# Pinning the background tasks of a decode step's forward and backward passes to their written place in each engine's order of issue

## The chip, the cores and the metric

The kernel runs on one core of one Trainium2 chip, in a single launch. The metric is the device time of one execution in microseconds (us). Each instruction stands in the queue of one engine (PE for matrix products, DVE for vector work, ACT for scalar work and activations, POOL, and SP, which here only issues transfers), and each engine takes its own queue strictly in the order in which the program was built. Engines wait for each other, and for transfers, by semaphores.

## The reference: what is computed

Two layers, A and B, are applied in turn, twice (A, B, A, B), to one row x of 1024 numbers, and then the gradients of everything are taken by the chain rule from a given `grad_out`. A is attention over a cache, with 32 query heads that share 4 groups of keys and values of 65536 positions each, 128 wide; B is a dense layer with a squared ReLU. Everything is in bfloat16. Cut to what matters:

```python
x = x + A(layernorm(x))      # q = x@wq; softmax(q k^T/sqrt(128)) v; @wo, 8 heads share a group
x = x + B(layernorm(x))      # relu(x@w1+b1)**2 @ w2 + b2
x = x + A(layernorm(x))      # the same caches and weights again
x = x + B(layernorm(x))
out, vjp = jax.vjp(f, x, k_cache, v_cache, wq, wo, w1, b1, w2, b2); grads = vjp(grad_out)
```

The caches are 67 MB each. Their gradients are as large, and are the bulk of what is written; the gradients of wq, wo, w1 and w2 are written too.

## The kernel before

The work over the caches falls into four passes. In passes 1 and 2 (`attn_fwd`) the keys and values are read for the two forward applications of A; in pass 3 (`attn_bwd3`) both are read again for the gradient of the second application; in pass 4 (`attn_bwd4`) they are read once more for the gradient of the first application, and the gradients of both caches, which need the sum over both applications, are formed and written. Between the passes stand the dense layers, which run over slabs of w1 and w2.

A pass goes over 4 groups of 64 items. An item is 8 blocks of 128 positions; four items share one loaded slab of K and one of V (1 MB each). `pipeline` (before: line 453) writes the stages of an item with lags: in pass 4, in round i, `vT` of item i (8 transposes on PE into `ps_tr`, line 875, evacuated by ACT line 151 or DVE line 154), `vS` of item i-2 (8 products into `ps_sc`, line 895; after each four items DVE and POOL form the tile X, lines 902 to 905, and PE transposes it, line 910), and `k8` of item i-7 (8 products for dq, line 932, and four products for the cache gradients, line 938, into the two buffers of `ps_gg`, evacuated by ACT or DVE through `evac` into one of three staging pairs; after four items POOL issues the two output transfers, lines 945 and 946). After the stages of round i, `pipeline` calls the background tasks that the dictionary `bg` holds for i.

The background tasks that matter here, with their written rounds in pass 4:

- `OutGrad.later` forms the dots of 8 rows of wo with a gradient, for a group to come: `dot_va` is a DVE product (line 379) and an ACT sum (line 380). For group 2 (in order) the rounds are 16, 21, ... 51, with rows fetched by SP; for group 3 they are 78, 82, ... 106, with rows fetched by ACT's own queue (line 676) 8 rounds earlier into three row buffers; for group 4 they are 136, 138, ... 150, fetched 4 rounds earlier in the same way.
- `QueryGrad.early` does the same with 8 rows of wq for each of three groups, from rounds 152, 175 and 202 on, with 2.75 rounds from dot to dot and the fetch (line 731) 5 rounds ahead. `QueryGrad.transposed` follows from round 226.
- `rows_ready` (line 1148) clears two row areas with POOL at round 72.
- The weight gradients: `rows_into` (lines 957 to 964) and units of `outer2` (one `ps_gg` buffer each, line 988, and an evacuation), spread evenly over rounds 73 to 252.

In pass 3 there are `OutGrad.later` with slabs that SP loads, `QueryGrad.early` and the transposition of w2; in passes 1 and 2, the rest of the queries and the output products of the groups.

The order that is written is not the order that is issued. A scheduler reorders the instructions when the program is built: it issues what it holds to be ready, the earlier written first, and it keeps only what the data demand. A background task can therefore stand far ahead of its round on an engine's queue. In the built program of before, all 24 steps of `OutGrad.later` in pass 4, with the 16 fetches that ACT issues, stand between instructions 528 and 634 of ACT's order, where pass 4 takes about 528 to 1110; their written rounds are 16 to 150 of 256. Slots for slabs come from `ring`, and a load waits on SP until the slot's last reader is done.

Of the kernel before, what the change touches and what calls it, by code (L numbers as in the profile page):

```python
# [18 lines left out]
def kernel(  # L19
# [22 lines left out]
    out_9: bass.AP,  # L42
):
    nc = tc.nc
    D = A_x.shape[-1]
    G = A_k_cache.shape[1]
    SK = A_k_cache.shape[2]
# [4 lines left out]
    F = B_w1.shape[1]  # L52
    assert DH == P and D == 1024 and QD == 4096 and F % P == 0 and G == 4 and R == 8
    DC, FC = D // P, F // P
    C = SK // P
# [242 lines left out]
    def ln_fwd(x, name):  # L298
# [3 lines left out]
        negmean = tmp.tile([P, 1], F32, name="ln_negmean")  # L302
        nc.vector.tensor_scalar(out=negmean[:], in0=tot[:, :], scalar1=-1.0 / D, scalar2=None, op0=ALU.mult)
        xc = tmp.tile([P, DC], F32, name="ln_xc")
# [6 lines left out]
        rstd = vec.tile([P, 1], F32, name=name + "_rstd")  # L311
        nc.scalar.activation(out=rstd[:], in_=tot2[:, :], func=ACTF.Sqrt, bias=eps_t[:], scale=1.0 / D)
        nc.vector.reciprocal(out=rstd[:], in_=rstd[:])
# [6 lines left out]
    def ln_bwd(dn, n, rstd):  # L320
# [6 lines left out]
        negm = tmp.tile([P, 2], F32, name="lnb_negm")  # L327
        nc.vector.tensor_scalar(out=negm[:], in0=tot[:, :], scalar1=-1.0 / D, scalar2=None, op0=ALU.mult)
        t = tmp.tile([P, DC], F32, name="lnb_t")
# [53 lines left out]
    class RowDots:  # L383
# [12 lines left out]
        def block(self, kc, view):  # L396
# [8 lines left out]
                "C": (L["dve"] + 0.15 * (ng + 1) + N * 0.00053, L["act"], L["pe"] + cpe),  # L405
                "D": (L["dve"] + 0.15, L["act"] + 0.19 * ng + N * 0.00081, L["pe"] + cpe),
            }
# [42 lines left out]
        return ap[:, i * 1024:(i + n) * 1024].rearrange("p (a b) -> p a b", b=P)  # L450


    def pipeline(n, stages, bg=None):
        maxlag = max(l for _, l in stages)
        for i in range(n + maxlag):
            for fn, lag in stages:
                if 0 <= i - lag < n:
                    fn(i - lag)
            for fn in (bg or {}).pop(i, ()):
                fn()  # L460
        assert not bg, sorted(bg)

    def items_of(order):
# [51 lines left out]
    def attn_fwd(L, order, eT, s_areas, more=None, keep=(), have=()):  # L515
# [75 lines left out]
        def v8(idx):  # L591
# [9 lines left out]
            if c8 + 8 == C:  # L601
                sl = slice(g * R, (g + 1) * R)
                nc.vector.tensor_tensor(out=L["oT"][:, sl], in0=ps_o[:, :, 0], in1=L["rZ"][:, sl], op=ALU.mult)
                nc.vector.tensor_copy(out=L["oTb"][:, sl], in_=L["oT"][:, sl])

        pipeline(n, [(kT, 0), (kS, TLEAD), (v8, LAGV)], bg)

    def mlp_hidden(L):
# [156 lines left out]
    def attn_bwd3(L, og, order, eT, dqT, bg):  # L765
# [46 lines left out]
        def k8(idx):  # L812
# [13 lines left out]
            if c8 + 8 == C:  # L826
                nc.vector.scalar_tensor_tensor(out=dqT[:, g * R:(g + 1) * R], in0=ps_dq[:, 0, :], scalar=SCALE,
                                               in1=L["rZ"][:, g * R:(g + 1) * R], op0=ALU.mult, op1=ALU.mult)

        pipeline(n, [(vT, 0), (vS, TLEAD), (k8, TLEAD + UB // 8 + 1)], bg)  # L830

    def attn_bwd4(La, Lb, oga, ogb, order, eTa, eTb, dqT, bg, group_done, streams):
# [82 lines left out]
        def k8(idx):  # L915
# [31 lines left out]
            if c8 + 8 == C:  # L947
                nc.vector.scalar_tensor_tensor(out=dqT[:, g * R:(g + 1) * R], in0=ps_dq[:, 0, 0:R], scalar=SCALE,
                                               in1=La["rZ"][:, g * R:(g + 1) * R], op0=ALU.mult, op1=ALU.mult)
                group_done(order.index(g))  # L950

        pipeline(n, [(vT, 0), (vS, TLEAD), (k8, TLEAD + UB4 // 8 + 1)], bg)


# [281 lines left out]
```

## Time and profile before

| what | us |
|---|---|
| time, median of 3 runs | 2064.12 |
| lowest and highest run | 2061.42, 2067.66 |
| the profiled execution, its own time | 2065.97 |
| its span, first to last instruction | 2064.2 |
| PE, DVE, ACT, POOL busy | 1622.7, 1123.7, 1025.3, 187.8 |
| passes 1 and 2, by the profile about | 12 to 418, 428 to 774 |
| pass 3, about | 832 to 1200 |
| pass 4, about | 1261 to 2040 |

809.62 MB move in all, at a mean of 392 GB/s over the span. The page gives busy time by engine, then the span in 40 equal slices, then the chain of work that ended last: it is followed back from the last instruction, at each step to what released it. A line such as "DVE pair L379 <- DMA pair<-in_A_wo_dram: 20.6, 5, 4.9" says that the DVE instructions of line 379 sat idle 20.6 us in 5 waits, the longest 4.9, until a transfer had landed. In a table of stretches the columns are the stretch, its length, the busy time of PE, its weight loads, DVE, ACT and POOL (instructions in brackets), the granted clock of PE as a share of full speed, the mean busy share of the 16 transfer engines, and the rate that they moved.

### The profile page before, as it was taken

The page shows a single profiled execution, that of the slowest core. Times are in us where ns is not written, and L with a number is a line of the kernel's source. Part 1 is how long each engine was busy: PE and PEld are TensorE (multiplying, and loading weights), DVE is VectorE, ACT ScalarE, POOL GpSimd, SP SyncE. Part 2 cuts the span into 40 slices and gives each one's busy share as a digit, 9 for nine tenths or more (in the row PEclk, how much of TensorE's full clock was granted, in tenths as well). Part 3 has the DMA queues.
Part 4 walks back from the last instruction along what each step waited for, and adds up shares of the span by engine and source line. Part 5 has one row for each costly group of instructions (what it writes and reads, how often), then busy time and mean ns, then how long its engine had stood idle before and what let it go on. Part 6 is the DMA issues. An engine that isn't in the chain of part 4 may idle for free.

```text
span 2064.2 us, 66060 instructions
## 1 busy us (share of the span) xinstructions
PE 1622.7 (79%) x29884; PEld 1332.7 (65%) x29884; DVE 1123.7 (54%) x1817; ACT 1025.3 (50%) x1276; POOL 187.8 (9%) x334
## 2 busy tenths in 40 slices
PE   7888887689888756887787766677888887887886
PEld 7878776578887646877676664455555554555553
DVE  4543431255434304745435557567876766777775
ACT  4543432225433403334435547667665755767764
POOL 0000000000000000000000002112222222222222
PEclk9998997579999955899999977989999988999997
DMA  9999999999999997899999996989999999999996
GB/s 384 419 419 416 414 419 410 390 374 418 415 418 416 400 417 282 359 417 418 416 419 391 413 372 258 362 326 425 424 424 407 405 425 383 398 357 415 394 421 250
DMA packets 142414, 809.62 MB, mean 392 GB/s; under 512 B 14132, under 2 KB 14132, under 8 KB 60980
## 3 DMA queue, kind: packets, MB, share of 16 engines
q1 hardware_dynamic: 108372, 627.12, 75.0%
q0 software_dynamic: 26848, 165.69, 19.6%
q10 hardware_dynamic: 6912, 12.59, 1.7%
q8 instruction: 234, 3.83, 0.7%
q14 instruction: 48, 0.39, 0.0%
HBM read 639.64 MB, written 165.69 MB: 390 GB/s over the span
## 4 chain that ended last, share of the span: by engine, by line
DMA 36%; PE 32%; ACT 15%; DVE 10%; issue 5%; SPq 0%; POOL 0%; ACTq 0%; DVEq 0%; POOLq 0%
DMA slot<-in_A_k_cache_dram 8%; DMA out_dram<-pair 7%; DMA slot<-in_A_v_cache_dram 5%; ACT small L151 5%; PE ps_tr L537 4%; PE ps_sc L556 4%; PE ps_tr L781 3%; DMA pair<-in_A_wq_dram 3%; ACT pair L151 3%; DMA pair<-in_A_k_cache_dram 3%; PE ps_gg L938 3%; PE ps_tr L875 2%; PE ps_acc L599 2%; DMA pair<-in_B_w_dram 2%; DVE small L154 2%
## 5 line engine op out<-in xcount | busy, mean ns | idle before, releaser
L154 DVE COPY small<-ps_tr 128x1024 bf16<-128x1024 bf16 x659 | 444.6, 687 | 347.1 <-PE ps_tr L537 171.9
L151 ACT COPY small<-ps_tr 128x1024 bf16<-128x1024 bf16 x381 | 380.9, 1014 | 415.1 <-PE ps_tr L537 231.7
L151 ACT CAST pair<-ps_gg 128x1024 bf16<-128x1024 f32 x292 | 293.3, 1017 | 164.2 <-PE ps_gg L938 126.1
L154 DVE CAST pair<-ps_gg 128x1024 bf16<-128x1024 f32 x220 | 268.5, 1221 | 80.5 <-PE ps_gg L938 61.0
L938 PE MATMUL ps_gg<-slot,small 64*128 64x512 bf16 x1024 | 199.3, 404 | 72.8 <-DVE pair L154 49.1
L556 PE MATMUL ps_sc<-L_qpad,small 128*128 128x64 bf16 (+7 forms) x3712 | 173.4, 193 | 25.9 <-ACT small L151 11.9
L537 PE MATMUL ps_tr<-ident_b,slot 128*128 128x128 bf16 x2304 | 160.7, 222 | 15.6 <-DMA slot<-in_A_k_cache_dram 13.4
L875 PE MATMUL ps_tr<-ident_b,slot 128*128 128x128 bf16 x1696 | 155.7, 229 | 15.7 <-DVE small L154 10.6
L556 PEld LDWEIGHTS <-small 128*128 128x128 bf16 x3712 | 138.8, 99 | 43.1 <-ACT small L151 20.3
L599 PE MATMUL ps_acc<-eT,slot 128*128 128x64 bf16 x2720 | 131.0, 210 | 38.6 <-DMA slot<-in_A_v_cache_dram 36.6
L875 PEld LDWEIGHTS <-slot 128*128 128x128 bf16 x1696 | 107.9, 102 | 68.1 <-issue 54.8
L537 PEld LDWEIGHTS <-slot 128*128 128x128 bf16 x2304 | 135.0, 99 | 18.7 <-DMA slot<-in_A_k_cache_dram 16.3
L599 PEld LDWEIGHTS <-slot 128*128 128x128 bf16 x2720 | 115.3, 107 | 43.0 <-DMA slot<-in_A_v_cache_dram 40.7
L938 PEld LDWEIGHTS <-small 64*128 64x128 bf16 x1024 | 60.3, 94 | 117.1 <-issue 85.7
L537 PE MATMUL ps_tr<-ident_b,pair 128*128 128x128 bf16 x1600 | 115.8, 226 | 11.3 <-DMA pair<-in_A_k_cache_dram 11.3
L802 PE MATMUL ps_sc<-B_dOpad,small 128*128 128x64 bf16 (+7 forms) x2048 | 102.1, 194 | 23.7 <-ACT small L151 16.1
L895 PE MATMUL ps_sc<-DOB,small 128*128 128x64 bf16 (+3 forms) x2048 | 120.1, 197 | 0.0
L895 PEld LDWEIGHTS <-small 128*128 128x128 bf16 x2048 | 93.1, 101 | 41.7 <-issue 35.1
L537 PEld LDWEIGHTS <-pair 128*128 128x128 bf16 x1600 | 97.1, 102 | 14.6 <-DMA pair<-in_A_k_cache_dram 13.2
L802 PEld LDWEIGHTS <-small 128*128 128x128 bf16 x2048 | 79.1, 100 | 39.0 <-ACT small L151 24.9
L562 DVE TENSOR_REDUCE pm_all<-pair 128x8 f32<-128x512 f32 x64 | 43.9, 686 | 108.0 <-ACT pair L561 108.0
L988 PE MATMUL ps_gg<-pair 128*128 128x512 bf16 x240 | 79.3, 411 | 25.8 <-ACT pair L151 19.5
(265 smaller groups left out, 2392.6 us busy)
## 6 DMA issues: line engine op xcount, KB each, us to landing
slot<-in_A_v_cache_dram SPq DMA_DIRECT2D x172, 1024.0 KB, 13.8
slot<-in_A_k_cache_dram SPq DMA_DIRECT2D x160, 1024.0 KB, 19.6
out_dram<-pair POOLq DMA_DIRECT2D x128, 1024.0 KB, 15.6
pair<-in_A_k_cache_dram SPq DMA_DIRECT2D x81, 1024.0 KB, 19.4
pair<-in_A_v_cache_dram SPq DMA_DIRECT2D x76, 1024.0 KB, 19.8
out_dram<-eT POOLq DMA_DIRECT2D x44, 512.0 KB, 14.9
slot<-in_A_wo_dram SPq DMA_DIRECT2D x16, 1024.0 KB, 10.9
slot<-in_A_wq_dram SPq DMA_DIRECT2D x18, 768.0 KB, 10.5
```

Source lines behind the costliest of these rows:

```text
L151: nc.scalar.copy(out=out, in_=in_)
L154: nc.vector.tensor_copy(out=out, in_=in_)
L537: nc.tensor.transpose(pt[:, i, :], kb8[:, i, :], ident_b[:, :])
L556: nc.tensor.matmul(ps_s[:, slot:slot + w, :].rearrange("p a b -> p (a b)"), lhsT=kt[:, i, :], rhs=L["qpad"][:, g, 0:w, :].rearrange("p a b ...
L562: nc.vector.tensor_reduce(out=pm_all[:, :, c0 // UB], in_=S_sb[:, :, c0:c0 + un], axis=AX.X, op=ALU.max)
L599: nc.tensor.matmul(ps_o[:, :, :].rearrange("p a b -> p (a b)"), lhsT=vb8[:, i, :], rhs=eT[g][:, :, c:c + 8], start=(c == 0), stop=(c == C ...
L781: nc.tensor.transpose(pt[:, i, :], vb8[:, i, :], ident_b[:, :])
L802: nc.tensor.matmul(ps_dp[:, slot:slot + w, :].rearrange("p a b -> p (a b)"), lhsT=vt[:, i, :], rhs=dOpad[:, g, 0:w, :].rearrange("p a b -> ...
L875: nc.tensor.transpose(pt[:, i, :], vb8[:, i, :], ident_b[:, :])
L895: nc.tensor.matmul(ps_dp[:, slot:slot + w, :].rearrange("p a b -> p (a b)"), lhsT=vt[:, i, :], rhs=DOB[:, g, 0:w, :].rearrange("p a b -> p ...
L938: nc.tensor.matmul(pg[:, t2 * 512:(t2 + 1) * 512], lhsT=xt[64 * t2:64 * t2 + 64, blk0 + half, :], rhs=GG[64 * t2:64 * t2 + 64, :, :, :].re ...
L988: nc.tensor.matmul(pg[:, q0:q0 + qq], lhsT=av[:, kb + kk, :], rhs=b_rows[:, n0 + m0 + q0:n0 + m0 + q0 + qq], start=True, stop=True)
```

## The change

A background task is no longer called directly by `pipeline` but through `in_order`. That function notes how many instructions were traced, runs the task, and looks back (over at most 4000 instructions) for the last instruction traced before the task on each engine that the task uses. The first instruction of the task on each such engine gets an edge to that one, of a kind that fixes the order of issue and adds no semaphore wait. The rest of the task, and the stages of later items, are free as before: they may still be issued ahead of the task. No instruction is added or taken away, and every evacuation stays on the engine that it was on.

```diff
+    NOSYNC = mybir.DependencyInfo(mybir.DependencyClass.NoSync, mybir.DependencyReason.DATA)
...
+    def in_order(fn):
+
+        insts = nc.cur_bb.bb.instructions
+        n0 = len(insts)
+        before = {}
+        fn()
+        new = list(insts[n0:])
+        want = {i.engine for i in new}
+        k = n0 - 1
+        while want - set(before) and k >= max(0, n0 - 4000):
+            before.setdefault(insts[k].engine, insts[k])
+            k -= 1
+        for i in new:
+            p = before.pop(i.engine, None)
+            if p is not None:
+                tc.add_manual_dep(i, p.name, NOSYNC, reason="in_order")
+
     def pipeline(n, stages, bg=None):
...
             for fn in (bg or {}).pop(i, ()):
-                fn()
+                in_order(fn)
```

The transfers that a task issues are instructions of the issuing engine's queue, and are pinned with it: the row fetches on ACT's queue, those on SP's, and the clearing on POOL's.

## The prediction, as it was put on record before the result was known

> **What bounds the kernel now.** I read the 40 slices of the page first, then a table of stretches of pass 4, then the chain of waits in the stretch that stood out, then who waited for whom there, and last the order of issue of the two programs as built.
>
> The slices (rows: busy share of the transfer engines, and their rate in GB/s):
>
> ```profile
> DMA  9999999999999997899999996989999999999996
> GB/s 384 419 419 416 414 419 410 390 374 418 415 418 416 400 417 282 359 417 418 416 419 391 413 372 258 362 326 425 424 424 407 405 425 383 398 357 415 394 421 250
> ```
>
> The transfer engines are busy nearly everywhere, at 414 to 425 GB/s when nothing disturbs them. The bytes do not change, so a gain can only come from where the rate is lower: slices 24 to 26, where pass 4 starts, and some of 31 to 39. Passes 1 and 2 have the same order in both programs, so their dips stay.
>
> Pass 4 in stretches (columns: length, busy PE, weight loads, DVE, ACT, POOL with counts, clock, transfer share, GB/s):
>
> ```profile
> 1256.00:1376.00 120.00, 84.85 (x1140) 58.87 (x1139) 79.62 (x130) 82.95 (x108) 25.48 (x37) 0.84 0.78 292
> 1376.00:1480.00 104.00, 85.26 (x1295) 58.32 (x1293) 83.70 (x119) 73.00 (x78) 23.18 (x41) 1.00 1.01 419
> 1480.00:1580.00 100.00, 84.98 (x1089) 55.81 (x1089) 71.29 (x86) 68.14 (x70) 27.30 (x49) 0.97 1.01 424
> 1580.00:1640.00 60.00, 51.88 (x666) 33.81 (x666) 46.97 (x69) 40.27 (x43) 14.40 (x26) 0.94 0.98 393
> 1640.00:1720.00 80.00, 61.23 (x756) 39.88 (x756) 53.41 (x70) 48.34 (x55) 17.01 (x31) 0.90 1.01 424
> 1720.00:1760.00 40.00, 32.45 (x397) 20.97 (x395) 28.68 (x44) 23.98 (x29) 8.94 (x15) 0.86 0.95 370
> 1800.00:1860.00 60.00, 49.94 (x600) 31.52 (x596) 46.25 (x70) 38.56 (x44) 12.85 (x23) 0.89 0.94 352
> 1900.00:1940.00 40.00, 31.77 (x386) 20.11 (x386) 27.42 (x33) 26.95 (x31) 10.72 (x19) 0.91 0.98 385
> ```
>
> From 1376 to 1580 and 1640 to 1720 the rate is at its ceiling, 419 to 424, with DVE and ACT at 60 to 80%: the transfers bound pass 4 there. From 1256 to 1376 they move 292 GB/s with no engine full: something makes all of them wait. The chain of waits names it (start, length, what):
>
> ```profile
> 1293.52 9.53 DMA pair<-in_A_wo_dram
> ...
> 1307.29 7.78 DMA pair<-in_A_wo_dram
> ...
> 1323.36 7.09 DMA slot<-in_A_wo_dram
> ...
> 1333.44 8.20 DMA pair<-in_A_wo_dram
> ...
> 1345.52 10.40 DMA pair<-in_A_wo_dram
> ...
> 1363.30 8.88 DMA slot<-in_A_wo_dram
> ```
>
> Six row fetches of wo, 51.9 us of the 80 from 1296 on. They are fetches of `OutGrad.later` for groups 3 and 4, written for rounds 70 to 146 and issued by ACT right at the start. Only three row buffers exist, so each fetch follows the dot that frees a buffer, and DVE's next dot waits for the fetch. The evacuations queued behind the dot on DVE and ACT wait with it, then PE, then the slots, then the loads. Who waited, from 1256 to 1376 and from 1700 to 2030 (idle us, times, longest):
>
> ```profile
> DVE pair L379 <- DMA pair<-in_A_wo_dram: 20.6, 5, 4.9
> DVE slot L379 <- DMA slot<-in_A_wo_dram: 4.6, 3, 3.8
> ```
>
> ```profile
> DVE pair L379 <- DMA pair<-in_A_wq_dram: 32.0, 8, 5.7
> DVE slot L379 <- DMA slot<-in_A_wq_dram: 4.1, 3, 2.7
> ```
>
> The second pair is the same with the rows of wq, which are hoisted by only a few rounds.
>
> **The change, part by part.** The sum is made against the profiled execution, 2065.97 us (span 2064.2), which is 1.9 above the median of the runs, 2064.12.
>
> *The start of pass 4.* In the new order the 24 wo dots leave positions 528 to 634 of ACT's queue for 550 to 845, that is their written rounds 16 to 150; the 16 fetches on ACT's queue move with them, 4 to 8 rounds ahead of their dots. A round takes about 3.0 us (256 from 1261 to 2030), so a fetch has 12 us or more. The pieces above are 7.1 to 10.4 long: it lands in time, and the waits go. What is late next is the transfers: 120 us at 292 GB/s are 35.0 MB, which at 424 need 82.6, so at most 37.4 can go. Of these, 16.5 lie at 1266 to 1286, where the finer table shows 54 and 95 GB/s: all slots are full and SP waits up to 28.2 us for PE to finish the first slab (line 875). That is compute, not waiting for rows; but ACT is busy 9.5 of 10 us there and six of the dots take 6 x 1.23 of it (1.04 for the sum and 0.19 to read it), so I take 5. From 1296 to 1376 the mean is 334 GB/s, 26.7 MB: 63 us at 424, so 17 can go, and I take 16. The lower end is the time in which the transfer engines were idle from 1296 on, their missing busy shares: 8.9. **Start: -21, bounds -8.9 to -37.**
>
> *The wq dots.* Their order moves later by 3 to 24 places on ACT, so a fetch gets its written 5 rounds, 15 us, where the issue-to-landing row of those fetches says 5.2 to 9.6. The 36.1 us of DVE's waits should go. But transfers ran on beneath most of them. What was lost by rate from 1580 to 2020 is 4.4 + 5.1 + 1.3 + 10.2 + 0.4 + 3.7 + 1.7 = 26.8 (each stretch times 1 minus its rate over 424), of which 20.7 lie between 1720 and 1940. In those stretches PE is busy 79 to 83%, after each wait even above 90%: part of the dip is the catching up, part plain work of the weight gradients (line 964's seven copies, 4.2 us on the chain at 1832), which stays. I take half. **wq: -10, bounds 0 to -26.8.**
>
> *What the dots cost where they land.* 16 dots of 0.69 on DVE and 1.23 on ACT, 30.7 us of engine time, go to rounds 78 to 106 and 136 to 150, about 1495 to 1580 and 1670 to 1710. Both stretches run at 424 GB/s with ACT at 60 to 68%: the transfers hide them. In the second there is a dot every other round, beside the weight gradients, and half of 8 x 1.23 may show. If the cover were gone, all would. **+4, bounds 0 to +30.7.**
>
> *The lag of the cache gradients.* Between items 145 and 217 the new order puts the transposes of `vT` 13 to 15 items ahead of the same item's line 938, where it was 9 to 10, and the dq products 6 to 10 ahead, where it was 2 to 3. K slots come free earlier, outputs go later: 5 items of 0.52 MB, 2.6 MB or 6 us if they could not be caught up; from item 224 the lag is 8 again. **0, bounds -6 to +6.**
>
> *The rest.* `rows_ready` moves from place 22 to 86 on POOL; its 3.5 us memset delays one pair of copies (line 904): 0, at most 3.5. In pass 3 SP issues one 1 MB slab of wo behind four K and V loads instead of before, and eight DVE dots stand some 2 to 15 places later, while the rate is back at 419 from 850 on: 0, within 2 either way. PE's weight-gradient products keep their place among line 938's. No instruction is added.
>
> Sum: -21 - 10 + 4 = -27: 2039 for the profiled execution, **2037** for the median.
>
> A rule of the Trainium skill speaks against the change. The rows: the waits go because fetches are issued later, at round 70 instead of from 1266 us on. "Perfetto Trace Analysis", section "Identifying the Most-Contended Engine", says to find what the engine's gaps wait on and make those dependencies start sooner or finish faster. By it, later fetches would lengthen waits, and the 25.2 us of waits for wo would come back in rounds 70 to 150; by the rows, it is the dots that stand too early, and the waits are gone. The same page, section "Roofline", gives about 120% of 358 GB/s as one core's practical ceiling, an estimate of 430; the trace shows 424 to 425, and by 430 the start could give 38.6 instead of 37.4.
>
> **The rivals.**
>
> *Hidden anyway.* While DVE waited, the transfer engines were 92% busy from 1296 to 1376. If that rate was low because of what was transferred, only the idle share comes back: -8.9 + 4, wq nothing: about 2059 (2054 to 2064). For it: the share; against it: 424 GB/s on the same kinds of load and store right after.
>
> *The dots meet a full chain: slower.* Place: rounds 78 to 150. There each item needs two of the two `ps_gg` buffers and the weight gradients up to one more. If the chain of fill and evacuation is as slow as the transfers, each dot in front of an evacuation holds it for its own time: +30.7, against -21 or only -8.9, and the wq waits stay since their fetches now sit behind the lagging evacuations on ACT: 2074 to 2086, say 2080. It decides once more than about 21 of the 30.7 shows. For it: PE 85% busy there and the lag in the order; against it: ACT 60 to 68%.
>
> *All the lost rate comes back.* -37 and -21 to -27, and some work no longer bunched: 2005 to 2020, say 2010.
>
> That the edges do nothing is excluded by the order: they hold only the first instruction of a task on an engine, but the dots and fetches do move.
>
> **How the numbers follow.** Forecast, 2022 to 2052: 0.60. Hidden: 0.15. Slower: 0.12. All back: 0.13. 0.3% is 6.2 us, about what a measurement here can tell. Faster than 2058: 0.60 + 0.13 + a third of 0.15 = 0.78. Same: the rest of it and a fifth of the slower case: 0.12. Slower: 0.10. The range leaves out the slower case and half of the best: 2015 to 2064.
>
> **What would show it.** Right: no wo row on the chain at the start of pass 4, DVE's waits for wo and wq under some 10 us in all, 400 or more GB/s from about 1290 on, ACT's wo dots spread over rounds 16 to 150. Wrong: waits for wo rows between rounds 70 and 150, rates under 400 there with DVE or ACT above 85%, or wq waits as long as before.

## The result, and the profile after

The changed kernel takes 2049.01 us (median of 4 runs, 2045.81 to 2051.04), the kernel before 2062.77 (4 runs, 2060.91 to 2067.66): a ratio of 0.9928, with a 95% interval of 0.9905 to 0.9951. It is faster by 0.7%. The forecast was 2037, a gain of 1.3%: the direction holds, the range holds the time, and the gain is about half of what was expected. The profiled execution of the changed kernel is its fastest, 2045.81 with a span of 2044.0, and that of before is 3.2 above its median. So the two traces differ by 20.2 us where the medians differ by 13.8; what follows compares traces with traces and medians with medians.

The slices of the page after:

```profile
DMA  9999999999999997899999998799999999989996
GB/s 384 418 419 415 415 419 411 391 372 419 416 418 415 415 404 290 345 419 416 415 420 384 368 383 335 315 424 424 409 419 423 414 417 415 409 353 416 422 420 260
```

Counted from 1 (the prediction counted from 0), slices 25 and 26 (about 1226 to 1329 us) still hold a dip, but from slice 27 on the rate is 409 or more, except in slice 36 and the last. Slices 22 and 23, the end of pass 3, are lower than before: 384 and 368 where they were 391 and 413.

Pass 4 after, in stretches (columns as before: length, busy PE, weight loads, DVE, ACT, POOL, clock, transfer share, GB/s):

```profile
1260.00:1300.00 40.00, 31.62 (x499) 23.65 (x498) 30.02 (x60) 26.70 (x31) 8.23 (x14) 0.88 0.54 209
1300.00:1380.00 80.00, 67.53 (x1071) 46.23 (x1069) 63.19 (x78) 63.34 (x72) 19.99 (x34) 1.00 1.01 419
1380.00:1480.00 100.00, 77.53 (x1082) 52.19 (x1084) 72.36 (x109) 64.20 (x69) 24.38 (x38) 0.95 1.01 417
1480.00:1580.00 100.00, 84.38 (x1104) 55.62 (x1114) 77.56 (x108) 70.19 (x79) 25.02 (x45) 0.95 1.01 421
1640.00:1720.00 80.00, 61.82 (x764) 40.16 (x769) 55.80 (x81) 51.24 (x64) 17.93 (x32) 0.87 1.01 415
1720.00:1820.00 100.00, 81.17 (x1025) 53.53 (x1035) 74.85 (x106) 69.29 (x83) 23.18 (x41) 0.91 1.01 415
1820.00:1840.00 20.00, 18.27 (x200) 11.44 (x202) 17.67 (x29) 10.48 (x13) 3.31 (x5) 0.76 0.66 245
1840.00:1940.00 100.00, 81.59 (x936) 49.94 (x945) 70.42 (x85) 73.58 (x85) 23.23 (x42) 0.86 1.02 419
```

From 1300 to 2000 the transfers run at 414 to 421 GB/s (the stretches not shown, 1580 to 1640 and 1940 to 2000, included), with one hole of 20 us at 1820; behind 2000 the pass runs out. The stretch that moved 334 GB/s before (1296 to 1376) moves 418 now.

The chain of waits after, between 1300 and 1660, its pieces above 9 us (start, length, what):

```profile
1321.10 17.66 DMA out_dram<-pair
...
1348.18 19.96 DMA out_dram<-pair
...
1377.67 21.13 DMA out_dram<-pair
...
1403.18 15.54 DMA slot<-in_A_v_cache_dram
...
1422.46 17.14 DMA slot<-in_A_v_cache_dram
...
1493.03 23.55 DMA out_dram<-pair
...
1528.39 25.36 DMA out_dram<-pair
...
1601.17 23.80 DMA out_dram<-pair
...
1642.42 9.47 DMA pair<-in_A_wo_dram
```

The six fetches of wo that stood at its start are gone. What is there now is the output transfers and the cache loads themselves, which is what a stretch at its ceiling looks like. One row fetch is left, at 1642, beside group 4's dots. DVE's waits for rows, from 1256 to 2030 (idle us, times, longest), are one line:

```profile
DVE pair L380 <- DMA pair<-in_A_wo_dram: 5.9, 1, 5.9
```

There were 25.2 us for wo and 36.1 for wq; none for wq is left.

Where did the rest of the gain go? I timed the passes by the same instructions in both traces: pass 3 from the first transposes of `vT` to the first product that uses the transposed w2, pass 4 from its first transposes to its last product with the transposed wq.

| | pass 3 | gap to pass 4 | pass 4 | span |
|---|---|---|---|---|
| before | 384.0 | 44.8 | 781.4 | 2064.2 |
| after | 391.4 | 42.9 | 756.3 | 2044.0 |
| difference | +7.4 | -1.9 | -25.1 | -20.2 |

The last 0.6 us lie ahead of pass 3 and behind pass 4. Pass 4 gained nearly the 27 that were forecast for it. Pass 3, which I had set at nothing, lost 7.4. There, in the stretch 1080 to 1210, where the dots of wq for three groups stand, the rate fell (columns as above); before:

```profile
1080.00:1210.00 130.00, 98.46 (x1996) 89.14 (x1993) 70.18 (x110) 65.16 (x91) 0.00 (x0) 0.93 1.01 403
```

and after:

```profile
1080.00:1210.00 130.00, 96.38 (x1946) 87.11 (x1944) 65.89 (x98) 63.37 (x87) 0.00 (x0) 0.93 0.96 376
```

27 GB/s over 130 us are 3.5 MB, or 8.3 us at 424: the whole loss of pass 3. No engine does more work. Who made SP, which issues the loads, wait (1090 to 1210) says why; before:

```profile
SPq L248 <- PE ps_tr L781: 37.6, 16, 5.0
SPq L248 <- ACT slot L380: 28.6, 9, 5.2
```

and after:

```profile
SPq L249 <- ACT slot L381: 62.0, 8, 10.1
SPq L249 <- PE ps_tr L799: 13.8, 7, 5.8
```

`QueryGrad.early` in pass 3 takes three dots from one slab of wq, and each dot has a round of its own, two rounds after the last. Before, the three were issued close together: from 1100 to 1200 the third ACT sum of a slab starts 2.1 to 3.0 us after the first. Pinned, it comes four rounds after the first, some 6 us at 1.5 us a round (384.0 over 256); the trace has 6.0 to 9.4. The slab's slot is held until then, the next load that `ring` gives that slot waits at the head of SP's queue, and the loads behind it wait with it. One slab before (start, length, what), first the sums on ACT, then SP's issues:

```profile
1120.11 1.06 ACT L380 ACTIVATE slot<-slot 128x1024 bf16<-128x1024 bf16 x1 [1.36 <-DVE slot L379]
...
1122.06 1.06 ACT L380 ACTIVATE slot<-slot 128x1024 bf16<-128x1024 bf16 x1
...
1123.11 1.04 ACT L380 ACTIVATE slot<-slot 128x1024 bf16<-128x1024 bf16 x1
```

```profile
1118.68 0.33 SPq L248 DMA_DIRECT2D slot<-in_A_wq_dram  x1
1124.27 0.33 SPq L248 DMA_DIRECT2D slot<-in_A_v_cache_dram  x1
...
1125.70 0.50 SPq L248 DMA_DIRECT2D slot<-in_A_k_cache_dram  x1
1129.34 0.33 SPq L248 DMA_DIRECT2D slot<-in_A_v_cache_dram  x1
```

The same after, ACT:

```profile
1119.24 1.06 ACT L381 ACTIVATE slot<-slot 128x1024 bf16<-128x1024 bf16 x1 [1.36 <-DVE slot L380]
...
1121.39 1.06 ACT L381 ACTIVATE slot<-slot 128x1024 bf16<-128x1024 bf16 x1
...
1126.91 1.06 ACT L381 ACTIVATE slot<-slot 128x1024 bf16<-128x1024 bf16 x1
1127.87 0.19 ACT L381 ACTIVATION_READ_ACCUMULATOR slot<-slot 128x1 f32 x1
```

and SP:

```profile
1118.73 0.40 SPq L249 DMA_DIRECT2D slot<-in_A_k_cache_dram  x1
1119.23 0.39 SPq L249 DMA_DIRECT2D slot<-in_A_wq_dram  x1
1128.09 0.33 SPq L249 DMA_DIRECT2D slot<-in_A_v_cache_dram  x1
1128.47 0.90 SPq L1108 DMA_DIRECT2D pair<-in_B_w_dram  x2
1129.46 0.54 SPq L249 DMA_DIRECT2D slot<-in_A_k_cache_dram  x1
1130.10 0.38 SPq L249 DMA_DIRECT2D slot<-in_A_v_cache_dram  x1
...
1140.25 0.33 SPq L249 DMA_DIRECT2D slot<-in_A_k_cache_dram  x1
```

SP issues nothing from 1119.6 to 1128.09, which is 0.03 after ACT has read the sum; then a handful of loads leave within 4 us, and the next comes 8 us later. Before, SP issued something every 1 to 6 us here. That loads leave in bursts, and the transfer engines run dry between them, was a theory at this point. (In the last rounds of the pass the code also takes eight areas out of `ring`, line 1097 of before. Whether a slab held as long would cost anything with those slots still there was not tried.)

### The profile page after: what moved, and what is told of

Same layout as the page of the kernel before. It is cut to its first block, busy times and chain, and to the rows that moved or that the text cites. A ratio compares the mean times of both kernels' runs of the same rounds, so it can differ in the third digit from the quotient of the medians.

```text
span 2044.0 us, 65972 instructions
## 1 busy us (share of the span) xinstructions
PE 1615.9 (79%) x29820; PEld 1327.9 (65%) x29884; DVE 1119.6 (55%) x1817; ACT 1025.1 (50%) x1276; POOL 187.0 (9%) x334
## 5 line engine op out<-in xcount | busy, mean ns | idle before, releaser
L956 PE MATMUL ps_gg<-slot,small 64*128 64x512 bf16 x1024 | 201.5, 405 | 52.0 <-ACT pair L152 15.8
L555 PE MATMUL ps_tr<-ident_b,slot 128*128 128x128 bf16 x2304 | 162.5, 223 | 13.8 <-DMA slot<-in_A_k_cache_dram 11.5
L893 PE MATMUL ps_tr<-ident_b,slot 128*128 128x128 bf16 x1696 | 150.9, 225 | 13.9 <-DMA slot<-in_A_v_cache_dram 11.2
L617 PEld LDWEIGHTS <-slot 128*128 128x128 bf16 x2720 | 115.4, 107 | 42.9 <-DMA slot<-in_A_v_cache_dram 40.0
L381 ACT ACTIVATE pair<-pair 128x1024 bf16<-128x1024 bf16 (+1 forms) x68 | 79.5, 1169 | 33.4 <-DVE pair L380 30.0
## 6 DMA issues: line engine op xcount, KB each, us to landing
slot<-in_A_k_cache_dram SPq DMA_DIRECT2D x160, 1024.0 KB, 13.9
pair<-in_A_k_cache_dram SPq DMA_DIRECT2D x81, 1024.0 KB, 19.2
```

Source lines behind the costliest of these rows:

```text
L381: nc.scalar.activation(out=view, in_=view, func=ACTF.Copy, accum_out=ycol)
L555: nc.tensor.transpose(pt[:, i, :], kb8[:, i, :], ident_b[:, :])
L617: nc.tensor.matmul(ps_o[:, :, :].rearrange("p a b -> p (a b)"), lhsT=vb8[:, i, :], rhs=eT[g][:, :, c:c + 8], start=(c == 0), stop=(c == C ...
L893: nc.tensor.transpose(pt[:, i, :], vb8[:, i, :], ident_b[:, :])
L956: nc.tensor.matmul(pg[:, t2 * 512:(t2 + 1) * 512], lhsT=xt[64 * t2:64 * t2 + 64, blk0 + half, :], rhs=GG[64 * t2:64 * t2 + 64, :, :, :].re ...
```

## The experiments

Each ratio, with its 95% interval, is against the kernel before as it ran beside the experiment. Its median was 2064.57 (11 runs) beside each pass by itself, the wq dots of pass 3 not pinned and the wo dots of pass 4; 2063.21 (11) beside the two with a slab's three dots in one round; and 2062.78 (16) beside the other four.

**Each pass by itself.** The theory: pass 3's pins cost some 7 us and pass 4's bring about 25. The rival: pass 4 gains only the 14 to 20 of the whole, and pass 3's longer time is chance.

```diff
-    def pipeline(n, stages, bg=None):
+    def pipeline(n, stages, bg=None, pin=False):
...
-                in_order(fn)
+                in_order(fn) if pin else fn()
...
-        pipeline(n, [(vT, 0), (vS, TLEAD), (k8, TLEAD + UB4 // 8 + 1)], bg)
+        pipeline(n, [(vT, 0), (vS, TLEAD), (k8, TLEAD + UB4 // 8 + 1)], bg, True)
```

> Only the tasks of pass 4 are pinned; passes 1 to 3 are issued as before. Theory (pass 4 gains 25 us, pass 3 loses 7.4): the loss of pass 3 goes, so about 2037 to 2043 us median, 6 to 8 under the changed kernel's 2049, and the stretch from the first transposes of pass 3 to the products with w2 (pg2) is again 384 us instead of 391. Rival (pass 3's 7 us are chance or come from elsewhere): 2047 to 2051, and that stretch stays near 391.

Measured: 2039.05, 0.9878 [0.9860, 0.9896]. In the trace pass 3 takes 384.1, pass 4 756.6; the rate from 1080 to 1210 is back at 402 GB/s. Its interval lies wholly below that of the changed kernel (0.9905 to 0.9951): this version beats both kernels.

The same edit with `True` in `attn_bwd3` instead:

> Only the tasks of pass 3 are pinned; pass 4 is issued as before. Theory: pass 3 takes 391 instead of 384 us, and nothing else changes: 2068 to 2071 us against 2062.8. Rival (the slip of pass 3 is swallowed by the prefetch at the start of pass 4, or is chance): 2061 to 2065.

Measured: 2076.29, 1.0058 [1.0041, 1.0075]; pass 3 takes 395.9, pass 4 780.6. Pinning pass 3 costs 11.7 us, more than I expected. The two halves, -25.5 and +11.7, make -13.8, which is what the medians of the whole change differ by.

SP's wait for the last reader, in pass 3 alone pinned (1090 to 1210):

```profile
SPq L249 <- ACT slot L381: 68.3, 8, 11.8
```

**Only the wq dots of pass 3 not pinned.** Is it these dots, or the slab of wo and the transposition of w2, which are pinned in pass 3 too?

```diff
-                in_order(fn)
+                fn() if fn in free else in_order(fn)
```

where `free` holds the tasks of `QueryGrad.early` that have no row buffers, which are those of pass 3.

> All tasks pinned as in the changed kernel, except the wq dots of pass 3 (QueryGrad.early with slabs from the ring), which are called directly. Theory: these dots, issued later on DVE and ACT, hold their slab's slot longer, and SP, which must keep its order, waits for that slot with all loads behind it (62 us of waits for ACT's sums in the last group instead of 29). Free again, they give back the 7 us: 2038 to 2044, waits of SP for ACT line 380 near 30 us. Rival (the w2 transposes or the wo slab moved on SP's queue are the cause): 2046 to 2051, waits near 60.

Measured: 2039.53, 0.9881 [0.9864, 0.9897]; pass 3 takes 385.5, and SP waits for ACT 27.9 us. The wq dots alone are the loss of pass 3.

**All pinned, a slab's three dots in one round.** If the loss is the time for which a slab is held, the pins may all stay as long as the third dot comes soon after the first.

```diff
-                    at(bg, i0 + 1 + int((kc * len(gs) + i) * step), lambda kc=kc, i=i: one(kc, i))
+                    at(bg, i0 + 1 + int((kc * len(gs) + (i if rows is not None else 0)) * step), lambda kc=kc, i=i: one(kc, i))
```

> Everything pinned as in the changed kernel, but in pass 3 the three wq dots of one slab are written for the same round instead of two rounds apart, so that the slab's slot is held for a shorter time. Theory (the pins cost pass 3 its 7 us only through the slot that the last dot of a slab holds): pass 3 to the products with w2 takes 383 to 386 us, SP's waits for ACT's sums fall from 62 to near 30, 2038 to 2043. Rival (pinned dots delay the evacuations of pass 3, wherever they stand): 391 us for pass 3, 2046 to 2051.

Measured: 2041.93, 0.9889 [0.9869, 0.9909]; pass 3 takes 383.2, at 402 GB/s from 1080 to 1210. SP's waits there:

```profile
SPq L249 <- PE ps_tr L799: 42.0, 18, 5.7
SPq L249 <- ACT slot L381: 24.9, 9, 4.3
```

ACT's share is back from 62.0 to 24.9 and PE's to 42.0, near the 28.6 and 37.6 of before. The third sum of a slab now starts 2.1 us after the first. SP's waits in all hardly moved (93.3 us before, 89.0 after, 91.5 here); what moved is whether they come in many short pieces or, for two thirds of the time, in eight of up to 10.1 us. The theory is shown: every pin stays, only the hold of the slabs is undone, and the loss is gone.

The same edit with pass 4 alone pinned asks whether there is anything more to have:

> Pass 4 alone pinned, and the three wq dots of a slab of pass 3 written for one round as well. Theory (in the order of before these dots already stand close, the scheduler has moved them forward): the same as with pass 4 alone pinned, 2037 to 2042, pass 3 at 383 to 385. Rival (there is more to gain from slots freed early): under 2036.

Measured: 2040.64, 0.9884 [0.9865, 0.9903]. It is the same as pass 4 alone.

**The parts of pass 4.** Which of its pinned tasks bring the gain? First only the wo dots and their row fetches (`OutGrad.later`, groups 2, 3 and 4, those of group 2 with SP's fetches), nothing else in any pass:

```diff
-                in_order(fn)
+                in_order(fn) if fn in pinned else fn()
```

> Nothing is pinned but the wo dots and their fetches in pass 4. Theory (the start is worth some 16 us, the wq dots and the rest some 9): 2045 to 2050 us, the wo rows gone from the chain at the start of pass 4, DVE's waits for wq rows still near 36 us. Rival (the wo dots alone carry all of pass 4's gain): 2036 to 2041. Rival (they meet a full chain and give it back): 2058 or more.

Measured: 2050.71, 0.9936 [0.9918, 0.9953]; pass 4 takes 768.6, 12.8 less than before. DVE's waits for rows:

```profile
DVE pair L380 <- DMA pair<-in_A_wq_dram: 27.8, 9, 5.5
...
DVE slot L380 <- DMA slot<-in_A_wq_dram: 8.8, 3, 3.4
DVE pair L380 <- DMA pair<-in_A_wo_dram: 6.0, 2, 5.5
```

Then only the wq dots of pass 4, their fetches and the transposition of wq:

> Nothing is pinned but the wq tasks of pass 4 (QueryGrad.early and transposed, with their fetches). Theory (the two hoisted families of rows cost separate stalls; with the wo tasks alone pinned pass 4 was 12 us shorter, with everything 25): the other 10 to 13 us, 2051 to 2056 us, DVE's waits for wq rows near 0, those for wo still near 25. Rival (after the wo stall the slots are refilled, so the wq stalls matter only when the wo stalls are gone, or the pins on the weight gradients do it): 2060 to 2066.

Measured: 2055.21, 0.9960 [0.9948, 0.9972]; pass 4 takes 769.6, 11.8 less.

```profile
DVE pair L380 <- DMA pair<-in_A_wo_dram: 20.9, 6, 7.8
...
DVE slot L380 <- DMA slot<-in_A_wo_dram: 5.1, 2, 4.6
```

Each takes its own waits away, but for 6.0 us of wo, and leaves the other's. 12.8 + 11.8 = 24.6, where pinning all of pass 4 takes 24.8: the pins on the weight gradients and on `rows_ready` give nothing that the traces show. By the medians the two are 13.9 and 7.6, together 21.5 of 25.5, so up to 4 us may be theirs or the measurement's.

**Does the landing of the dots cost ACT time?** To pass 4 alone I added a second, useless ACT sum to each of the 16 wo dots of groups 3 and 4, into a spare column: 16 x 1.25 = 20 us more of ACT in the same rounds.

```diff
+                if queue is nc.scalar:
+                    junk = tmp.tile([P, 1], F32, name="junk")
+                    nc.scalar.activation(out=view, in_=view, func=ACTF.Copy, accum_out=junk[:])
```

> Pass 4 alone pinned, as in the run that gave 2039, and ACT forms the sum of each wo dot of groups 3 and 4 a second time into a spare column: 16 more activations of about 1.2 us, 20 us of ACT, in rounds 78 to 150. Theory of the prediction (the transfers hide the dots where they land, a few us at most show): 2039 to 2045. Rival (the evacuation chain is full there, each dot delays it by its own time): 2053 to 2059.

Measured: 2042.78, 0.9904 [0.9881, 0.9927]. That is 3.7 above pass 4 alone, within the intervals of the two, and pass 4 is 0.7 longer in the trace. ACT had room for it.

**Fetches too close to their dots.** Pass 4 alone, with the fetches of wo 2 rounds and 1 ahead of the dots instead of 8 and 4. This puts the waits for rows where the dots now stand.

```diff
-    og1.later(vbx1, ORD4[2], bg, IPG + 14, 4, wo_rows, 8, nc.scalar)
-    og1.later(vbx1, ORD4[3], bg, 2 * IPG + 8, 2, wo_rows, 4, nc.scalar)
+    og1.later(vbx1, ORD4[2], bg, IPG + 14, 4, wo_rows, 2, nc.scalar)
+    og1.later(vbx1, ORD4[3], bg, 2 * IPG + 8, 2, wo_rows, 1, nc.scalar)
```

> Pass 4 alone pinned, and the wo fetches on ACT's queue are written 2 rounds (group 3) and 1 round (group 4) ahead of their dots instead of 8 and 4: about 6 and 3 us, where a fetch needs 7 to 10 to its dot. Theory (a dot that waits for its row stalls the evacuations behind it, wherever it stands): DVE waits for wo rows 30 to 60 us in 16 waits, and 10 to 30 of it shows: 2050 to 2070. Rival (such waits are covered once the pass is under way, and the start of the pass was special): 2038 to 2043 with the same waits.

Measured: 2060.26, 0.9981 [0.9964, 0.9997]; pass 4 takes 777.9, 21.3 more than with the long leads. DVE's waits, and the stretches in which the dots stand:

```profile
DVE pair L380 <- DMA pair<-in_A_wo_dram: 32.3, 8, 5.8
...
DVE slot L380 <- DMA slot<-in_A_wo_dram: 11.7, 3, 5.3
```

```profile
1420.00:1500.00 80.00, 61.63 (x738) 39.45 (x742) 54.12 (x70) 47.07 (x53) 20.26 (x31) 0.86 0.98 399
1500.00:1580.00 80.00, 62.79 (x791) 41.08 (x800) 55.29 (x79) 53.19 (x59) 17.84 (x32) 0.95 0.97 377
1640.00:1720.00 80.00, 55.84 (x624) 36.56 (x629) 43.99 (x65) 44.08 (x53) 14.02 (x26) 0.76 0.90 350
```

The dots stand in their written rounds as in the changed kernel, and nearly all of the gain is lost: 44.0 us of waits for rows pull the rate down to 350 to 399 GB/s with no engine full. So it is the wait of a dot on DVE that costs, and not only at the start of the pass.

**Group 4's dots spread.** In pass 4 alone, items 128 to 144 (an item is timed by the first of its cache-gradient products, line 956), where eight dots stand in every other round, take 63 us where the 16 items on either side take 42 and 50. I spread them over rounds 112 to 140, one in four, fetched 8 ahead.

```diff
-    og1.later(vbx1, ORD4[3], bg, 2 * IPG + 8, 2, wo_rows, 4, nc.scalar)
+    og1.later(vbx1, ORD4[3], bg, IPG + 48, 4, wo_rows, 8, nc.scalar)
```

> Pass 4 alone pinned, and the 8 wo dots of group 4 are written for rounds 112 to 140, every fourth, with fetches 8 rounds ahead, instead of rounds 136 to 150, every second, with 4. Theory (items 128 to 144 took 63 us instead of 54 because the dots are dense there and one waits 5.8 us for its row): that stretch gives back part, 2032 to 2037. Rival (the stretch is longer only because 2 MB of rows are moved into it): 2038 to 2041.

Measured: 2042.75, 0.9904 [0.9886, 0.9922]: no gain. Items 128 to 144 fell to 50 us and items 112 to 128 rose from 42 to 52. No dot waited for its row any more (5.8 us with pass 4 alone), and that brought nothing either. My expectation missed and the rival held: the price went with the dots. Eight row fetches are 2.1 MB, 5 us at 420 GB/s. In this run the transfers move 419 to 423 GB/s from item 112 to item 144, so these bytes add their time in either place. That is half of the 10 us that moved; what the other half is was not shown.

## Why the prediction was right in direction and half wrong in size

**What bounds the kernel: right.** The start was held up by row fetches of wo, and with those gone it runs at 419 GB/s.

**The start of pass 4, -21: the 16 came, the 5 did not.** From 1296 to 1376 the rate is 418, so of the 17 us lost by rate all but 1 are regained. The 5 us of compute at 1266 to 1286 were not there to be had: SP's first long wait, for PE's transposes of the first slab, is 27.3 us where it was 28.2, and the 40 us around it still move 209 GB/s. Before (1256 to 1300; idle us, times, longest) and after:

```profile
SPq L248 <- PE ps_tr L875: 31.7, 2, 28.2
```

```profile
SPq L249 <- PE ps_tr L893: 27.3, 1, 27.3
```

Item 48, counted from the start of the pass, is reached 25.9 us sooner than before, which is more than 16 because some 10 of them are no gain by the bytes: 16 row fetches of 0.26 MB, 4.2 MB or 9.9 us at 424, have not been made yet and come later, in rounds where the transfers are full. (That is worked out; the spread of group 4's dots, where the price went with the rows, speaks for it.)

**What the dots cost where they land, +4: not settled.** Between items 48 and 144 the changed kernel takes 297.1 us where the kernel before took 282.7. Ten of these 14.4 are the postponed rows, which leaves about 4. But timed by the transposes of `vT` instead, the same items take 276.1 and 270.9, 5.2 more, and nothing is left; the cache gradients lag further behind there. What can be said is that it is not ACT's time, as I had it: 20 us more of ACT cost 0.7 to 3.7. Start and landing together, -17 by the prediction, are the wo dots alone: -12.8 in the trace, -13.9 in the medians.

**wq, -10: right.** All waits are gone, and the wq tasks alone bring 11.8 in the trace and 7.6 in the medians. So is the step that took half of the lost rate: the 26.8 us lost from 1580 to 2020 are down to 15.8 from 1580 to 2000. Of those, 8.4 are the hole at 1820, at `rows_into` and the setting up of group 4; the kernel before had a dip there as well (352 GB/s from 1800 to 1860). I did not try that place, and its cause stays open.

**The lag of the cache gradients and `rows_ready`, 0:** nothing in the sum calls for them; pass 4's parts add up to 24.6 of 24.8 without them. That the whole of pass 4 came within some 2 us of the -27 is in part luck: the wo dots brought 4 less than their -17, and wq in the trace 2 more than its -10.

**The rest, "0, within 2 either way": this is the step that failed.** Of pass 3 I had written that SP issues a slab of wo a few loads later and that "eight DVE dots stand some 2 to 15 places later". It measured +7.4 in the two traces (that of after is its fastest run, 3.2 under its median), +11.7 in the medians with pass 3 alone pinned. I looked at how far an instruction moved, and not at what it holds while it is late: the third dot of a slab of wq is the last reader of a slot, and the load that wants this slot stands at the head of SP's queue. In the medians, -25.5 for pass 4 and +11.7 for pass 3 make the whole; with 0 for pass 3 the time is 2039, as the first experiment shows, 2 from my forecast.

**The rivals.** *Hidden anyway* (2059) falls: the lost rate did come back, as pass 4 alone shows with 2039. (The 92% that spoke for it is 89% by the row of 1296 to 1376 in the trace of before, transfer share 0.89 at 334 GB/s.) *The dots meet a full chain* (2080) falls: twice the ACT sums, and hardly any change. *All the lost rate comes back* (2010) falls: from 1820 to 1840 it didn't, and the start is still bound by compute. The slower mechanism that does exist was none of my three: it was in the other pass.

**The rule that spoke against the change.** The Trainium skill, "Perfetto Trace Analysis", section "Optimization Strategy" (the prediction gave the section ahead of it), advises making what an engine waits on start sooner or finish faster. With the 16 fetches issued from 1425 to 1670 us, where before they were issued from 1266 to 1373, DVE's waits for wo fell from 25.2 to 5.9 us, so the measurement speaks against it here, where dot and fetch moved together and three buffers are shared. With the dots kept in place and the fetches only 2 rounds and 1 ahead the waits are 44.0: between a fetch and its own dot the rule holds.

## What to carry to other kernels

A background task that waits for its data is best issued when the data has landed, since everything behind it on an in-order queue waits with it: take the waits for its data out, and the transfers can use the time. But a pin also moves the last reader of a buffer, and if a load for that buffer is at the head of an in-order queue, a few microseconds of delay hold up all loads behind it; for each pinned task, ask which buffers it frees and who is next in line for them. Pin the pass whose traces show such waits (here pass 4 alone: 2039.05, which beats both kernels), and where several tasks share a loaded slab, put them in one round.

## What the runs showed of the hardware that was not expected

How long a row fetch takes seems to depend on what else is in flight. A landing is recorded for only a few of the 256 KB fetches of wo in pass 4. In the three traces in which these fetches stand at the held-up start (before, pass 3 alone pinned, the wq tasks alone), the six on record took 5.6 to 7.5 us from issue to landing. In the changed kernel and with pass 4 alone pinned, where the transfers run at 414 to 421 GB/s, the six on record took 8.9 to 11.1. But the six pieces on the chain of before, from a fetch to the dot that it held, are 7.1 to 10.4 us long at a mean rate of 334 GB/s, so the two ranges meet and a slower landing in a full stretch is suggested, not shown. For the lead the longest counts: the 12 us that the changed kernel leaves in group 4 were enough by little. One fetch there was late: it left ACT at 1642.42, just after the dot at 1641.64, and the dot that waited 5.9 us for it started at 1651.91.

And a wait is not worth its length. With the wo dots pinned, 19.2 us of DVE's waits for wo went (25.2 to 6.0) and pass 4 was 12.8 us shorter; the 36.1 for wq were worth 11.8; and the short leads added 38.2 (5.8 to 44.0) and cost 21.3. That is a third to two thirds, with whatever the moved dots cost where they land in it. While dots waited, the transfers went on at a lower rate: 334 GB/s from 1296 to 1376 before, 350 to 399 with the short leads.
